# Moving input loads behind the last raw weight pieces, and two pieces into another buffer, in a fused RWKV-7 and hard-swish kernel

## The chip, the cores and the metric

The kernel runs on one core of one Trainium2 chip. The metric is the device time of one execution in microseconds (us). Three runs of the kernel before took 801.73, 801.97 and 802.9 us, so the median is 801.97 us. Separately, one execution was profiled; the views below come from that one.

A core has five engines with an instruction queue each: TensorE (PE in the views; its weight loads appear as PEld), VectorE (DVE), ScalarE (ACT), GpSimd (POOL) and SyncE (SP), which here does nothing but issue DMA transfers. Engines run their own queue in order and wait for each other by semaphores.

## The reference

The recurrence over time of four batches with eight heads of size 40, and then a feed-forward layer on its outputs:

```
for t in range(S):                                   # S = 768
    y[:, :, t] = einsum('bhd,bhde->bhe', rt, state)
    Sa = einsum('bhde,bhe->bhd', state, at)
    state = state * wt - einsum('bhd,bhe->bhde', Sa, bt) + einsum('bhd,bhe->bhde', vt, kt)
x = y.transpose(0, 2, 1, 3).reshape(B * S, H * D)    # 3072 x 320
h = x @ w_in                                         # 320 x 2048
out = (h * clip(h + 3.0, 0.0, 6.0) / 6.0) @ w_out    # 2048 x 320
```

The inputs r, k, v, w, a, b have the shape (4, 8, 768, 40), all float32. `w_in` and `w_out` come to the kernel as 8-byte numbers, seen as pairs of 32-bit words, and are turned into float32 on the chip.

## The kernel before

**Units.** Time is cut into blocks of 64 steps (BL), and two batches are worked on together (the 128 partitions are 64 steps of each). One such piece is a *unit*; there are 24, four to a group (NU = 4), so units 0 to 3 are the first group, 4 to 7 the second. For each unit, `prepare(i, F)` gives the stages that don't need the recurrent state (W, gam, A, B, F, factor, K, E, EV), and `step(i)` those that do (RT, R, VT, S, U, C, UT, rS, sn, H, y, and move, move2, which copy the output to `xt`, the operand of the feed-forward layer). A group's four units write their 32 x 32 triangular parts into one buffer `F` (tag "F", two buffers); `invert` inverts a whole group at once on VectorE, row by row, and `third_block` completes the inverse with small matmuls. These read F and write `tinv`.

**Feed-forward.** `expand` (matmuls at L1058 into PSUM, then L1073 on ACT and L1074 on DVE) and `contract` (matmuls at L1099) are a stream of small portions. `pieces(n)` takes n of them and so mixes them into PE's order.

**Weights.** `load_weights` handles 20 pieces of `w_in` and `w_out`. A raw piece is loaded by SP (L328), then ACT computes the exponent's part in three steps (L351, L353, L355), DVE the mantissa's in two (L372, L376), and DVE's L363 multiplies the two into `win`, `win2` or `wout`. ACT's result goes to one of two buffers `parts` in turn. `raw_homes` yields the place of each raw piece, and in `free` the number of the piece that has to be converted first because it had that place. The places are: a and b, the halves of a buffer with tag "F"; c, d in `wout`, e, f in `win`, g, h in `tinv`; and "x", "fb", "tt", which the inversion uses too. `limit[0]` bounds how many pieces are loaded; it becomes 20 after line 3 of the plan.

**Order.** All engines' orders are written out by hand. For the first group's steps it is the text `PLAN`: each line names stages (0sn: stage sn of unit 0), and the number behind the colon says how many conversion steps are dealt out between its matmuls and its evacuation. P and Q are the stages W and gam of units 4 and 5. From line BEGIN = 10 on, the second group's preparation (`by_twos`) runs beside it.

**Loads.** `fetch(name, i)` issues the loads of an input of unit i: two DMAs of 80 KB for w, a, b, k (L460), four of 40 KB for r, v (L457). All but the very first go through SP, whose order is the order in which the program reaches the calls. Before the change, around the end of the first group's steps, SP's order is: R of unit 3 (called in RT of unit 2), raw pieces 13 and 14, `xt` of unit 0, V of unit 5 (called in gam of unit 5), raw piece 15, R of unit 4 (called in RT of unit 3), `xt` of unit 1, raw piece 16, V of unit 4, A of unit 5, W of unit 7 (the three called after plan line 8), raw pieces 17, 18, 19, the first half of `xt` of unit 2, B and K of unit 5, and the second half of that `xt`. Then come A of unit 6, A of unit 7, W of unit 8, `xt` of unit 3, B and K of units 6 and 7, and V of units 6 and 7.

Names of the views: a wait "L924 UT" is ACT's read of the stage UT's result from PSUM; "L902 U" that of the stage U; L934 are PE's matmuls of stage rS; L476 are PE's transposes of one input of one unit.

Of the kernel before, what the change touches and what calls it, by code (L numbers as in the profile page):

```python
# [8 lines left out]
F32 = mybir.dt.float32  # L9
I32 = mybir.dt.int32  # L10
U32 = mybir.dt.uint32
# [6 lines left out]
P = 128  # L18
BL = 64
# [12 lines left out]
def kernel(  # L32
# [42 lines left out]
    nc = tc.nc  # L75
    B, H, T, D = r.shape
# [3 lines left out]
    NU = 2 * NP  # L80
    DM, DFF = moe_w_in.shape
    NJ = DFF // P
    NH = NU * H
# [8 lines left out]
    inv = ctx.enter_context(tc.tile_pool(name="inv", bufs=1))  # L92
# [48 lines left out]
    def ps_pair(*dims):  # L141
# [21 lines left out]
        out=ident[:], in_=ones, pattern=[[1, P]],  # L163
# [4 lines left out]
        out=ones[:, 0:BL], in_=ones[:, 0:BL], pattern=[[1, BL]],  # L168
# [3 lines left out]
        out=ones[BL:P, 0:BL], in_=ones[BL:P, BL:P], pattern=[[1, BL]],  # L172
# [49 lines left out]
    for i in range(3):  # L222
        t = const.tile([P, H, BL], F32, name=f"score{i}")
# [48 lines left out]
    WC = 256  # L272
# [5 lines left out]
    def raw_homes():  # L278


        raws = inv.tile([P, NH, BL], F32, name="raw", tag="F", bufs=2)
        raws = raws[:].rearrange("p h t -> p (h t)").bitcast(U32)
        places = [raws[:, n * 4 * WC:(n + 1) * 4 * WC] for n in range(2)]
        for j in (NJ // 4, 3 * NJ // 4):
            places.append(wout[:, j:j + NJ // 4, :].rearrange("p j m -> p (j m)")[:, 0:4 * WC].bitcast(U32))
        places = [x.rearrange("p (n c t) -> p n c t", n=2, t=2) for x in places]
        for c in (DFF // 4, 3 * DFF // 4):
            x = win[:, :, c:c + 2 * WC].bitcast(U32)
            places.append(x.rearrange("p n (c t) -> p n c t", t=2))
        x = tinv[:].rearrange("p h t -> p (h t)").bitcast(U32)  # L290
        for n in range(2):
            y = x[:, n * 4 * WC:(n + 1) * 4 * WC]
            places.append(y.rearrange("p (n c t) -> p n c t", n=2, t=2))
        a, b, c, d, e, f, g, h = places
        order = [g, h, a, b, c, d, e, f, a, b, c, d, "x", "fb", "tt", a, b, "fb", "tt", a]
        free = [None] * 8 + [2, 3, 4, 5, None, None, None, 8, 9, 13, 14, 15]
        left = {}
        for n, (x, before) in enumerate(zip(order, free)):
            if isinstance(x, str):
                if x not in left:  # L300
                    left[x] = inv.tile([P, L, L], F32, name=f"raw_{x}", tag=x)
                x = left[x][:].rearrange("p t s -> p (t s)").bitcast(U32)
                x = x.rearrange("p (n c t) -> p n c t", n=2, t=2)
            yield x, before
# [221 lines left out]
    def prepare(i, F):  # L526
# [25 lines left out]
        def gam_stage():  # L552

            prods, wm = o["prods"], o["wm"]
            first = start[:].rearrange("p (n i) -> p n i", i=HB + 1)[:, :, 0]
            nc.vector.reciprocal(first, prods[:].rearrange("p r m i -> p (r m) i")[:, ::-1, HB])
            back = _ap(wm[:], SCAN, [[-1, SCAN]])
            nc.vector.tensor_tensor_scan(out=back, data0=back, data1=start[:], initial=0.0,  # L558
                                         op0=ALU.mult, op1=ALU.add)
            nc.vector.memset(first, 1.0)  # L560
            gam = o["G"] = grp.tile([P, NPR, P], F32, name="gam", tag="gam", bufs=NU + 2)
            rgam = o["rg"] = placed.get(("rgam", i)) or tmp.tile([P, NPR, P], F32, name="rgam", bufs=2)
            gv = gam[:].rearrange("p r (q i) -> p (r q) i", q=2)
            rv = rgam[:].rearrange("p r (q i) -> p (r q) i", q=2)
            row = 2 * (HB + 1)

            def copy(to, x):
                if i < NU:
                    nc.scalar.activation(out=to, in_=x, func=AF.Copy)
                else:  # L570
                    nc.vector.tensor_scalar(to, x, 1.0, None, ALU.mult)

            copy(gv[:, :, 0:HB], _ap(o["wm"][:], HB + 1, [[row, NB], [-1, HB]]))
            copy(rv[:, :, HB:BL], _ap(o["wm"][:], HB + 3, [[row, NB], [1, HB]]))
            nc.gpsimd.tensor_copy(gv[:, :, HB:BL], o["prods"][:, :, 1, 0:HB])  # L575
            nc.gpsimd.tensor_copy(rv[:, :, 0:HB], o["prods"][:, :, 0, 0:HB][:, :, ::-1])
            dec = grp.tile([P, 2, 2, NPR], F32, name="dec", tag="dec", bufs=NU + 2)
            nc.gpsimd.tensor_copy(dec[:].rearrange("p m q r -> p r q m"),
                                  o["prods"][:].rearrange("p (r q) m i -> p r q m i", q=2)[:, :, :, :, HB])
            o["dec"] = dec  # L580
            if NU < i <= 2 * NU:
                fetch("V", i)
            yield from ()

# [16 lines left out]
        def f_by_32():  # L601

            f = ps_pair(NPR, BL)
            for pr in range(NPR):
                for c in range(2):
                    for q in range(2):
                        for s in range(2):
                            x = q * BL + c * L
                            y = o["bt"][half(s, D), pr, half(q)].rearrange("p (c t) -> p c t", c=2)
                            if c:  # L610
                                y = y[:, ::-1, :]
                            z = (q ^ s) * BL + c * L
                            nc.tensor.matmul(out=f[s][z:z + L, pr, :],
                                             lhsT=o["at"][half(s, D), pr, x:x + L], rhs=y,
                                             start=True, stop=True, tile_position=(s * SLOT, z))
            yield PE
            nc.scalar.activation(out=F[:, n * H:n * H + H, :].rearrange("p (s r) t -> p s r t", s=2), in_=f[2],
                                 func=AF.Copy, scale=-1.0)

        def f_by_64():  # L620

            f = ps_pair(NPR, BL)
            for pr in range(NPR):
                for q in range(2):
                    for s in range(2):
                        nc.tensor.matmul(out=f[s][half(q ^ s), pr, :],
                                         lhsT=o["at"][half(s, D), pr, half(q)],
                                         rhs=o["bt"][half(s, D), pr, half(q)],
                                         start=True, stop=True)
            yield PE  # L630
            to = F[:, n * H:n * H + H, :].rearrange("p (s r) t -> p s r t", s=2)
            for z in range(0, P, BL):
                nc.scalar.activation(out=to[z:z + L, :, :, 0:L], in_=f[2][z:z + L, :, :, 0:L],
                                     func=AF.Copy, scale=-1.0)
                for c in range(2):
                    nc.scalar.activation(out=to[z + L:z + BL, :, :, c * L:c * L + L],
                                         in_=f[2][z + L:z + BL, :, :, L - c * L:BL - c * L],
                                         func=AF.Copy, scale=-1.0)
# [185 lines left out]
    def step(i):  # L824
# [8 lines left out]
        def s_RT():  # L833
            x = turn_in(o["RN"], halves)
            yield PE
            m["RT"] = turned("RT")
            for y, z in zip(parts_of(m["RT"], halves), x):
                nc.scalar.activation(out=y, in_=z, func=AF.Copy)  # L838
            if i:
                fetch("R", i + 1)  # L840
            if fresh:
                nc.gpsimd.tensor_copy(last_dec[p][:], dec[:, 1])
                return
            scale = tmp.tile([P, 2, NPR], F32, name="scale", bufs=2)
            nc.gpsimd.tensor_tensor(out=scale[:], in0=last_dec[p][:], in1=dec[:, 0], op=ALU.mult)
            nc.gpsimd.tensor_copy(last_dec[p][:], dec[:, 1])
            nc.vector.tensor_tensor(out=st[:, :, :, 0:D], in0=st[:, :, :, 0:D],
                                    in1=_ap(scale[:], 0, [[NPR, 2], [1, NPR], [0, D]]), op=ALU.mult)
# [314 lines left out]

    third, F, group_F = [], None, []

    def prepared(i):
        nonlocal F
        if i >= NK:
            return None
        if i % NU == 0:  # L1170
            F = inv.tile([P, NH, BL], F32, name="F", tag="F", bufs=2)
            group_F.append(F)
        return prepare(i, F)

    STAGES = 9
# [108 lines left out]
    for t, line in enumerate(plan):  # L1284
# [7 lines left out]
            limit[0] = PIECES  # L1292
        if t == BEGIN - 2:
            seconds()
            fetch("V", NU)
            fetch("A", NU + 1)
            fetch("W", NU + 3)
            third.clear()
            second_group = by_twos(NU, 3, 0, 1.25)
        if t == BEGIN + 1:  # L1300

            for name in "BK":
# [162 lines left out]
```

## Time and profile before

| what | value |
|---|---|
| median of 3 runs | 801.97 us (801.73 to 802.9) |
| profiled execution | 800.6 us, span 798.6 us |
| mean granted TensorE clock of that execution | 0.957 of full speed |
| DMA rate over the span | 56 GB/s; 174215 packets, 157424 of them under 512 bytes |
| the chain that ended last | PE 72%, DVE 13%, issue 5%, DMA 4%, SP's queue 4% |

The span is the time from the first to the last instruction in the trace; what lies around it is 2.0 us. Shares of busy time are means over stages with different limits. The first 165 us are a stage of their own (preparation of the first group, its inversion, its steps and the weights' conversion); from about 175 us PE works almost without a break. In the timelines, SPq rows are DMA issues: their duration is the time that SP was taken up by issuing, not that of the transfer.

### The profile page before, as it was taken

How to read it: one execution, taken by the hardware profiler on the slowest of the kernel's cores; microseconds unless marked ns; L12 is line 12 of the kernel's file. 1: busy time of each engine (PE TensorE's matmuls, PEld its weight loads, DVE VectorE, ACT ScalarE, POOL GpSimd, SP SyncE). 2: the span in 40 equal slices, each digit the busy share in tenths (PEclk: the TensorE clock that was granted, in tenths of full speed). 3: DMA queues.
4: the chain of work that ended last, by engine and by line, in shares of the span. 5: the costliest groups of instructions: out<-in, count | busy, mean ns of one | idle time of the engine just before them, and what ended most of it. 6: DMA issues, size and time to landing. Idle time of an engine off the chain costs nothing.

```text
span 798.6 us, 35318 instructions
## 1 busy us (share of the span) xinstructions
PE 731.4 (92%) x15832; PEld 621.3 (78%) x15832; DVE 495.9 (62%) x971; ACT 320.0 (40%) x664; POOL 174.7 (22%) x318
## 2 busy tenths in 40 slices
PE   5726686999999989999999999999999999999998
PEld 4625675878778878888888888888888888888886
DVE  7897975689545699445698445898444983322210
ACT  2357864321553424452334453324444324412111
POOL 6403110320222313223124123304222202000000
PEclk9855797999999999999999999999999999999999
DMA  9683552420323321233222223213222101110000
GB/s 123 120 199 94 133 145 65 77 42 9 54 49 70 62 49 36 47 62 59 41 43 45 44 57 63 52 28 60 43 49 48 24 16 29 30 29 9 14 19 17
DMA packets 174215, 45.03 MB, mean 56 GB/s; under 512 B 157424, under 2 KB 172784, under 8 KB 174064
## 3 DMA queue, kind: packets, MB, share of 16 engines
q1 hardware_dynamic: 169760, 42.03, 27.2%
q8 instruction: 125, 2.05, 1.0%
q10 hardware_dynamic: 4304, 0.74, 0.7%
q14 instruction: 26, 0.21, 0.1%
HBM read 34.08 MB, written 3.93 MB: 48 GB/s over the span
## 4 chain that ended last, share of the span: by engine, by line
PE 72%; DVE 13%; issue 5%; DMA 4%; SPq 4%; ACT 2%; POOL 1%; DVEq 0%; ACTq 0%; POOLq 0%
PE h L1058 24%; PE o L1099 22%; PE pair L514 4%; PE pair L976 3%; DVE prod L745 3%; DVE x L751 3%; PE pair L953 2%; PE pair L486 2%; PE one L476 2%; SPq L460 2%; PE pair L898 2%; SPq L457 2%; PE pair L860 2%; PE pair L934 1%; PE pair L918 1%
## 5 line engine op out<-in xcount | busy, mean ns | idle before, releaser
L1058 PE MATMUL h<-xt,win 128*128 128x128 f32 (+1 forms) x2304 | 249.4, 282 | 3.5 <-DVE gt L1074 3.3
L1058 PEld LDWEIGHTS h<-xt,win 128*128 128x128 f32 (+1 forms) x2304 | 230.0, 191 | 20.7 <-issue 4.6
L1099 PE MATMUL o<-wout,gt 128*128 128x320 f32 x768 | 230.8, 443 | 0.0
L1099 PEld LDWEIGHTS o<-wout,gt 128*128 128x128 f32 x768 | 138.7, 190 | 50.5 <-issue 0.4
L1074 DVE SCALAR_TENSOR_TENSOR gt<-gt,h 128x512 f32<-128x512 f32 x96 | 62.0, 680 | 72.0 <-ACT gt L1073 72.0
L1073 ACT ACTIVATE gt<-h,three 128x512 f32<-128x512 f32 x96 | 62.1, 685 | 97.6 <-PE h L1058 97.2
L988 POOL TENSOR_TENSOR yg<-ys,gam 128x512 f32<-128x512 f32 x22 | 39.0, 1772 | 157.8 <-DVE ys L987 75.0
L745 DVE TENSOR_TENSOR prod<-x 128x30 f32<-128x30 f32 (+9 forms) x180 | 67.2, 373 | 8.8 <-POOL x L730 3.3
L666 POOL TENSOR_TENSOR KBt<-K,rgt 128x320 f32<-128x320 f32 x22 | 19.1, 867 | 216.7 <-ACT rgt L655 205.6
L751 DVE TENSOR_TENSOR x<-x,prod 128x30 f32<-128x30 f32 (+9 forms) x180 | 62.2, 346 | 5.5
L961 DVE TENSOR_TENSOR state<-pair,state 40x320 f32<-40x320 f32 (+1 forms) x43 | 21.0, 488 | 63.5 <-PE pair L953 37.4
L522 DVE COPY_PREDICATED score<-mask,pair 128x512 f32<-128x512 int32 x72 | 50.5, 722 | 0.9 <-PE pair L514 0.4
L987 DVE TENSOR_TENSOR ys<-pair,ys 128x512 f32<-128x512 f32 x22 | 15.2, 690 | 44.4 <-PE pair L693 22.9
L558 DVE TENSOR_TENSOR_SCAN wm<-wm,start 128x528 f32<-128x528 f32 x24 | 37.5, 1563 | 0.8
L547 DVE TENSOR_TENSOR_SCAN prods<-wm,start 128x528 f32<-128x528 f32 x24 | 30.2, 1261 | 10.3 <-ACT wm L543 10.2
L838 ACT ACTIVATE RT<-pair 128x512 f32<-128x512 f32 x22 | 13.1, 596 | 53.8 <-PE pair L486 53.8
L698 ACT ACTIVATE EV<-pair 64x320 f32<-64x320 f32 x44 | 19.0, 431 | 33.0 <-PE pair L693 22.3
L813 ACT ACTIVATE tinv<-pair 32x256 f32<-32x256 f32 x48 | 18.0, 374 | 31.1 <-PE pair L803 30.5
L1117 ACT ACTIVATE ob<-o 128x320 f32<-128x320 f32 x22 | 9.6, 434 | 49.0 <-PE o L1099 24.8
L575 POOL COPY gam<-prods 128x256 f32<-128x256 f32 x24 | 22.0, 917 | 31.4 <-DVE prods L547 30.6
L976 PE MATMUL pair<-score,KBt 64*64 64x64 f32 x1408 | 26.2, 223 | 0.2 <-issue 0.2
L864 DVE TENSOR_TENSOR RR<-pair,EV 128x320 f32<-128x320 f32 x22 | 10.7, 486 | 25.3 <-PE pair L514 25.3
(264 smaller groups left out, 1078.0 us busy)
## 6 DMA issues: line engine op xcount, KB each, us to landing
V<-in_v_dram SPq DMA_DIRECT2D x96, 40.0 KB
out_dram<-ob SPq DMA_DIRECT2D x47, 80.0 KB
R<-in_r_dram SPq DMA_DIRECT2D x92, 40.0 KB
B<-in_b_dram SPq DMA_DIRECT2D x42, 80.0 KB
K<-in_k_dram SPq DMA_DIRECT2D x42, 80.0 KB
W<-in_w_dram SPq DMA_DIRECT2D x37, 80.0 KB
A<-in_a_dram SPq DMA_DIRECT2D x37, 80.0 KB
xt<-yg SPq DMA_DIRECT2D x72, 40.0 KB
```

Source lines behind the costliest of these rows:

```text
L514: nc.tensor.matmul(out=o[i][half(q), n, :], lhsT=lhs[half(i, D), n ^ (2 * q * swap), half(q)], rhs=rhs[half(i, D), n, half(q)], start=True ...
L522: nc.vector.copy_predicated(out=x[:].rearrange("p (i h) t -> p i h t", i=2), mask=mask8, data=o[2])
L547: nc.vector.tensor_tensor_scan(out=prods[:].rearrange("p r m i -> p (r m i)"), data0=wm[:, 0:SCAN], data1=start[:], initial=0.0, op0=ALU.m ...
L558: nc.vector.tensor_tensor_scan(out=back, data0=back, data1=start[:], initial=0.0, op0=ALU.mult, op1=ALU.add)
L745: nc.vector.tensor_tensor(out=pv, in0=_ap(x[:], (i + 1) * L + i, [[L, n], [0, i]]), in1=_ap(x[:], i * L, [[0, n], [1, i]]), op=ALU.mult,)
L751: nc.vector.tensor_tensor(out=rest, in0=rest, in1=pv, op=ALU.add)
L976: nc.tensor.matmul(out=y[q][half(s), pr, :], lhsT=o[name][half(q), h * D:h * D + SLOT], rhs=m[name][half(q), 4 * rs + 2 * s + j, :], start ...
L988: nc.gpsimd.tensor_tensor(out=yg[:], in0=m["ys"][:].rearrange("p r q t -> p r (q t)"), in1=o["G"][:], op=ALU.mult)
L1058: nc.tensor.matmul(out=hp[c][:, i, :], lhsT=lhsT, rhs=rhs, start=(begun[c] == 0), stop=(begun[c] == 3 * NQ - 1))
L1073: nc.scalar.activation(out=gt[:], in_=hp[c][:], func=AF.Relu, bias=three[:], scale=1.0)
L1074: nc.vector.scalar_tensor_tensor(out=gt[:], in0=gt[:], scalar=6.0, in1=hp[c][:], op0=ALU.min, op1=ALU.mult)
L1099: nc.tensor.matmul(out=op[:], lhsT=gts[c][:, n, :], rhs=wout[:, c * HJ + r * NQ + n, :], start=((split or r == 0) and c == 0 and n == 0), ...
```

## The change

The places of pieces 15 to 19 were a, b, fb, tt, a, with the last three waiting for pieces 13, 14 and 15 to be converted. They become a, b, F0, F1, fb: the two halves of the first group's F, without a wait for another piece, and then fb, after piece 13. Four loads of inputs are taken from where they were and called after plan line 10 (A of unit 5, W of unit 7) and after plan line 12 (V of units 4 and 5, R of unit 4). So that the first group's F can still be named when the pieces are loaded, the second group's F is no longer allocated when its preparation is set up, but at its first use (`lazy_F`).

```diff
-        order = [g, h, a, b, c, d, e, f, a, b, c, d, "x", "fb", "tt", a, b, "fb", "tt", a]
-        free = [None] * 8 + [2, 3, 4, 5, None, None, None, 8, 9, 13, 14, 15]
+        order = [g, h, a, b, c, d, e, f, a, b, c, d, "x", "fb", "tt", a, b, "F0", "F1", "fb"]
+        free = [None] * 8 + [2, 3, 4, 5, None, None, None, 8, 9, None, None, 13]
...
-            if isinstance(x, str):
+            if isinstance(x, str) and x[0] == "F":
+                x = group_F[0][:].rearrange("p h t -> p (h t)").bitcast(U32)[
+                    :, int(x[1]) * 4 * WC:(int(x[1]) + 1) * 4 * WC]
+                x = x.rearrange("p (n c t) -> p n c t", n=2, t=2)
+            elif isinstance(x, str):
...
-            if NU < i <= 2 * NU:
+            if NU + 1 < i <= 2 * NU:
                 fetch("V", i)
...
-            nc.scalar.activation(out=F[:, n * H:n * H + H, :].rearrange("p (s r) t -> p s r t", s=2), in_=f[2],
+            nc.scalar.activation(out=F()[:, n * H:n * H + H, :].rearrange("p (s r) t -> p s r t", s=2), in_=f[2],
                                  func=AF.Copy, scale=-1.0)
...
-            if i:
+            if i and i != NU - 1:
                 fetch("R", i + 1)
...
+    def lazy_F():
+        made = []
+
+        def get():
+            if not made:
+                made.append(inv.tile([P, NH, BL], F32, name="F", tag="F", bufs=2))
+                group_F.append(made[0])
+            return made[0]
+        return get
+
     def prepared(i):
...
         if i % NU == 0:
-            F = inv.tile([P, NH, BL], F32, name="F", tag="F", bufs=2)
-            group_F.append(F)
+            F = lazy_F()
         return prepare(i, F)
...
         if t == BEGIN - 2:
             seconds()
-            fetch("V", NU)
+            third.clear()
+            second_group = by_twos(NU, 3, 0, 1.25)
+        if t == BEGIN:
             fetch("A", NU + 1)
             fetch("W", NU + 3)
-            third.clear()
-            second_group = by_twos(NU, 3, 0, 1.25)
+        if t == BEGIN + 2:
+            fetch("V", NU)
+            fetch("V", NU + 1)
+            fetch("R", NU)
```

SP's order after the change is: `xt` of unit 0, raw piece 15, `xt` of unit 1, raw pieces 16, 17, 18, 19, A of unit 5, W of unit 7, the first half of `xt` of unit 2, B and K of unit 5, the second half of that `xt`, V of units 4 and 5, R of unit 4, A of unit 6, and from there on as before. The orders of instructions on PE, ACT, DVE and POOL stay as they were, apart from the buffers that the conversion of pieces 17 to 19 reads.

More of the change, by code (lines that the diff above doesn't have):

```diff
@@ L630, in f_by_64 @@
             yield PE
-            to = F[:, n * H:n * H + H, :].rearrange("p (s r) t -> p s r t", s=2)
+            to = F()[:, n * H:n * H + H, :].rearrange("p (s r) t -> p s r t", s=2)
             for z in range(0, P, BL):
```

## The prediction

> **What bounds the kernel now.** I read the page first (busy shares, the 40 slices), then the timeline of each engine between 78 and 205 us, where the changed issues lie, then the stretches of 2 us with their granted clock.
>
> ```profile
> PE 731.4 (92%) x15832; PEld 621.3 (78%) x15832; DVE 495.9 (62%) x971; ACT 320.0 (40%) x664; POOL 174.7 (22%) x318
> ...
> PE   5726686999999989999999999999999999999998
> ```
>
> TensorE (PE) sets the time, and nearly all that it does not work lies in the first seven slices of 20 us. From 300 to 700 us the stretches show it busy 98.7 to 100%. So a microsecond won on PE's path before 170 us stays won, unless something else holds PE up between there and the dense part. The issues of the diff lie at 96 to 119 us. PE's timeline there (start, us, what; in brackets the idle time before it and what ended it):
>
> ```profile
> 86.90 2.41 PE L976 MATMUL lent<-score,KBt 64*64 64x64 f32 x64 [1.91 <-DVE state L961]
> ...
> 104.47 0.69 PE L934 MATMUL pair<-RT,S 40*64 40x64 f32 x32
> ...
> 112.01 1.16 PE L1058 MATMUL h<-xt,win 128*128 128x128 f32 x8 [2.68 <-DVE gt L1074]
> ...
> 116.86 4.04 PE L1058 MATMUL h<-xt,win 128*128 128x128 f32 x40
> 127.42 1.13 PE L934 MATMUL pair<-RT,S 40*64 40x64 f32 x32 [6.52 <-ACT UT L924]
> ```
>
> The longest hole is the 6.52 us up to 127.42: PE waits for ScalarE (ACT) to read UT. ACT's timeline says why that is late:
>
> ```profile
> 113.57 0.78 ACT L351 ACTIVATE parts<-raw,low 128x512 int32<-128x512 int16 x1 [1.76 <-DMA raw<-in_moe_w_out_dram]
> ...
> 115.77 0.42 ACT L902 ACTIVATE U<-pair 128x320 f32<-128x320 f32 x1
> 120.28 0.77 ACT L351 ACTIVATE parts<-raw_fb,low 128x512 int32<-128x512 int16 x1 [4.10 <-DMA raw_fb<-in_moe_w_out_dram]
> ...
> 126.79 0.58 ACT L924 ACTIVATE UT<-pair 128x512 f32<-128x512 f32 x1
> ```
>
> ACT converts the raw weight pieces 16 to 19 in program order ahead of UT, and waits 1.76 us for piece 16 and 4.10 us for piece 17. Those were issued late, since SyncE's queue (SPq) issues without a pause from 82 to 122 us:
>
> ```profile
> 96.33 2.68 SPq L457 DMA_DIRECT2D V<-in_v_dram  x4
> 99.11 0.54 SPq L328 DMA_DIRECT2D raw<-in_moe_w_out_dram  x1
> 99.76 2.61 SPq L457 DMA_DIRECT2D R<-in_r_dram  x4
> ...
> 108.65 0.53 SPq L328 DMA_DIRECT2D raw<-in_moe_w_out_dram  x1
> 109.22 3.36 SPq L457 DMA_DIRECT2D V<-in_v_dram  x4
> 112.69 1.27 SPq L460 DMA_DIRECT2D WA<-in_a_dram  x2
> ...
> 115.42 0.57 SPq L328 DMA_DIRECT2D raw_fb<-in_moe_w_out_dram  x1
> ...
> 128.65 1.72 SPq L460 DMA_DIRECT2D B<-in_b_dram  x2
> ...
> 137.86 1.34 SPq L460 DMA_DIRECT2D A<-in_a_dram  x2
> ...
> 153.33 1.57 SPq L460 DMA_DIRECT2D K<-in_k_dram  x2
> ```
>
> The reader is to see that one issue costs SP 0.6 to 0.85 us whatever it carries, so the loads of V, R, A and W stand ahead of the raw pieces by their count.
>
> **The change, part by part.** No instruction is added to or taken from PE, ACT, VectorE (DVE) or GpSimd (POOL), and their order is the same; a few carry other waits. Only SP's order and two buffers differ.
>
> *Earlier pieces.* From start to start, V of unit 5 holds SP 2.78 us (96.33 to 99.11), R of unit 4 2.66 (99.76 to 102.42), V of unit 4 3.47 (109.22 to 112.69), A of 5 and W of 7 together 2.73 (112.69 to 115.42). Piece 16 now has the first two no longer ahead: 108.65 - 5.44 = 103.21. Piece 17 has all four gone: 115.42 - 11.64 = 103.78, and piece 18 0.67 behind it. Their new home, the first group's F, is free: its last reader, the third block's matmuls (L780), ended at 76 us. In the old homes they would have waited until pieces 13 and 14 were converted, 105.65 and 108.71. Piece 19 takes the home of 13 and so issues at 105.7 to 107.8. Piece 16 landed 4.83 us after its issue (108.65 to ACT's start less the 0.09 us between), and three pieces crossed between 117 and 122.6 us, under 2 us each. So the four land by about 108, 109.5, 111 and 113 (estimate from these rows).
>
> *ACT.* L1073 ends at 111.80 and piece 16 is there: L351 starts 1.76 us earlier and its third step ends near 114.1. The next, U (L902), needs PE's L898, which ends at 114.71, so U ends at 115.13 rather than 116.19. Piece 17 starts there rather than at 120.28: 5.15 us earlier. Three pieces at the 2.17 us that they take now (120.28 to 126.79) bring UT to 121.64. DVE keeps up: piece 16's last step, held up beside POOL's L988 as now, ends near 117.2, which is when ACT wants that buffer; each later piece costs DVE 0.43 + 0.69 + 0.69 = 1.81 us, under ACT's 2.17. **PE's L934 starts at about 122.27: -5.15 us**, and PE's hole shrinks to about 1.9 us.
>
> *The clock.* The granted clock in the stretches (columns: span, PE, PEld, DVE, ACT, POOL busy with counts, clock, DMA share, GB/s):
>
> ```profile
> 86.00:88.00 2.00, 1.10 (x32) 0.95 (x32) 2.00 (x4) 1.25 (x3) 1.48 (x4) 0.65 0.37 57
> ...
> 110.00:112.00 2.00, 0.00 (x0) 0.00 (x0) 1.13 (x3) 1.81 (x4) 0.00 (x0) 1.00 0.78 242
> ...
> 126.00:128.00 2.00, 0.58 (x20) 0.58 (x24) 1.65 (x3) 1.97 (x5) 0.00 (x0) 0.50 0.00 0
> ```
>
> After the hole of 6.52 us the clock stays at 0.50 until about 134.4 us (the stretch 134 to 136 has 0.90), so L934 takes 1.13 us rather than the 0.69 of 104.47. A hole of 1.91 us (to 86.90) also halved it, until 93 us; one of 2.68 us (to 112.01) did not. So for a hole of 1.9 us both can come. Halved again, PE takes the 9.98 us from 127.42 to the transposes at 137.40 as now. At full clock, by the full-clock rows of the same work (0.51 + 0.91 + 0.67 + 1.27 + 1.0 + 2.35 = 6.7), 3.3 us more are gained: -8.4 in all. [...]
>
> *The moved loads.* V of 4 and 5 and R of 4 (12 issues) now stand behind xt of unit 2 and ahead of A of unit 6 and all that follows; A of 5 and W of 7 fall before 116 us, where SP would idle until POOL's yg, and cost nothing. The 12 cost 2.78 + 2.66 + 3.47 = 8.91 us. Now SP needs 26.25 us from B at 128.65 to the end of K of unit 7 at 154.90, of which 3.54 us (134.32 to 137.86) is waiting for PE. Without that and with the 12: 26.25 - 3.54 + 8.91 = 31.6. B, which waits for L934, starts 5.15 earlier, at 123.5; K of unit 7 is issued by 155.1, 0.2 us later than now. PE reads it at 162.20 now, at 157.05 if shifted by 5.15. So it must land in 1.95 us. The trace has no clean landing time for such a load: from below, the 1.95 us that the chain gives to an xt copy; from above 3.2 us after the end of its issue (the load of A at 2.96 us landed 3.81 after its start, with the DMA engines full). I take 2.2, nearer the low end, since the DMA share is 0.1 to 0.5 around 150 us. That is a wait of 0.25 us; the ends give 0 and 1.25. B of unit 7 is read 1.8 us earlier and issued 1.6 to 1.8 earlier, so it waits about as long. V of 4 and 5 are read at 157.04 (now), R of 4 at 199: both landed long before.
>
> *Sum:* -5.15 + 0.25 = -4.9; with the clock full the same loads stop PE, at 162.20 - (154.5 + 2.2) = -5.5. I take **-5.2 us**. The 30 us chain of DVE (168 to 199 us) and PE's own work beside it begin from this PE work and move with it. The profiled execution took 800.6 us (span 798.6 and 2.0 around it): 795.4. The three runs have the median 801.97, 1.4 above it; the forecast for the median is 801.97 - 5.2 = **796.8 us**.
>
> **Rivals.**
> - *The loads keep up and the clock stays full*: -8.4, 793.6 us. For: the hole of 2.68 us that kept the clock. Against: K of unit 7 would have to be there at 153.8. By the issue cost of the first V loads (6.00 us for 8) and the shortest A, B, K pairs (1.27), SP saves at most 2 us.
> - *SP's backlog eats more of it*: PE, stopped for K or B of unit 7, halves its clock once more and pays up to 3.3 us. -1.9, 800.1 us. For: holes near 2 us did so at 86.90. Against: these holes would be about 1 us, in dense work.
> - *The gain is hidden*: DVE's inversion chain or a later load ends at the same time as now; 802.0 us. For: that chain is on the path from 168 to 202 us. Against: it starts from L613 and F of the same PE work.
> - *Slower: the queue is late.* If the 12 moved issues are long, K of unit 7 comes later than today. It decides from a landing at 162.2, that is an issue end 4.9 us later than worked out, at 8.91 + 4.9 = 13.8 us for 12, 1.15 each. The longest V issue in the trace took 1.50: 12 x 1.50 = 18.0, 9.1 more, landing at 166.4: +4.2, 806.2 us. For: that one row, behind a raw piece. Against: the median V issue, 0.62, and the next slowest group at 0.9 each.
>
> **How the numbers follow.** Forecast 0.62 (own range 795.3 to 798.3: the landing bounds and 0.4 us of scatter), clock full with loads in time 0.10, backlog 0.16, hidden 0.07, slower 0.05. A run of this kernel tells 0.2%, 1.6 us, from no change. The first three are faster by more than that, except a part of the backlog's upper end (0.02): faster 0.86, same 0.09, slower 0.05. The range reaches to the first rival and to the backlog: 793.4 to 800.3.
>
> **What would show it.** Right: the waits of L351 for raw pieces gone, L924 near 121.6, the hole before L934 under 2.5 us, SP busy without a break from 123 to 155, PE's transposes of K and B of unit 7 near 157 with a wait under 1.5 us. Wrong: piece 17 still waited for; issues of V and R above 1 us; the gap to today closing between 150 and 205 us.

## The result and the profile after

The changed kernel takes 798.56 us in the median of 18 runs (794.62 to 802.72); the kernel before, run beside it on the same chip, 801.91 us (798.76 to 803.48). The ratio is 0.9961, 95% interval 0.9947 to 0.9975: 3.35 us faster, by the interval's ends 2.0 to 4.25. The forecast was 796.8 us, 5.2 us faster. The direction held, but about a third of the forecast gain is missing. The time lies in the stated range (793.4 to 800.3), which took in two of the rivals; it lies just outside the forecast case's own range (795.3 to 798.3).

The profiled execution took 801.08 us (span 799.0), more than 16 of the other 17 runs, so its span must not be set against the median. It was also late before the change acts: at 66 us ACT's conversion step is 0.44 us later than in the profile of before, at 88 us 0.86, at piece 14, about 107 us, 1.15. To compare traces, I therefore count from the start of ACT's first step for piece 14 (L351 before, L355 after: the change adds four lines above it, so the lines named in the prediction are 4 higher here). The busy shares and the 40 slices of the profile after:

```profile
PE 734.8 (92%) x15832; PEld 624.2 (78%) x15832; DVE 495.9 (62%) x971; ACT 320.2 (40%) x664; POOL 174.7 (22%) x318
...
PE   5726788999999989999999999999999999999998
```

The instruction counts are the same; the sixth and seventh slice (100 to 140 us) went from 6 and 9 to 8 and 9. The place where ACT waited for raw pieces, in ACT's timeline after:

```profile
114.05 0.76 ACT L355 ACTIVATE parts<-raw,low 128x512 int32<-128x512 int16 x1
...
119.19 0.44 ACT L906 ACTIVATE U<-pair 128x320 f32<-128x320 f32 x1 [2.87 <-PE pair L902]
119.52 0.77 ACT L355 ACTIVATE parts<-F,low 128x512 int32<-128x512 int16 x1
...
126.08 0.58 ACT L928 ACTIVATE UT<-pair 128x512 f32<-128x512 f32 x1
```

Both waits for pieces (1.76 and 4.10 us) are gone, and pieces 17 to 19 run without a gap. In their place ACT waits 2.87 us in U for PE's L902. PE's timeline says why that is late, and what follows; the first line is the same group of matmuls in the profile of before, the others are from after:

```profile
114.08 0.63 PE L898 MATMUL pair<-RR,tinv 64*64 64x40 f32 x32
```

```profile
108.34 1.81 PE L1062 MATMUL h<-xt,win 128*128 128x128 f32 x17
111.89 1.19 PE L1062 MATMUL h<-xt,win 64*128 64x128 f32 x7 [1.75 <-issue]
114.36 2.08 PE L1062 MATMUL h<-xt,win 128*128 128x128 f32 x8 [1.28 <-DVE gt L1078]
116.37 1.99 PE L980 MATMUL pair<-score,KBt 64*64 64x64 f32 x64
118.13 0.92 PE L902 MATMUL pair<-RR,tinv 64*64 64x40 f32 x32
...
126.71 0.69 PE L938 MATMUL pair<-RT,S 40*64 40x64 f32 x32 [2.37 <-ACT UT L928]
...
160.13 0.63 PE L480 MATMUL pair<-ident,B 128*128 128x128 f32 x4 [1.44 <-DMA B<-in_b_dram]
```

The hole of 6.52 us shrank to 2.37. But there is a new hole of 1.75 us at 110 us, put down to "issue", that is to nothing that the profile shows; the eight L1062 matmuls after it take 2.08 us (1.16 before), because the clock has halved (0.50 in the stretch from 112 to 114 us, shown further down). And PE waits 1.44 us for B of unit 7. SP's queue after:

```profile
103.24 0.53 SPq L332 DMA_DIRECT2D raw<-in_moe_w_out_dram  x1
103.81 1.05 SPq L332 DMA_DIRECT2D F<-in_moe_w_out_dram  x2
106.50 0.92 SPq L332 DMA_DIRECT2D raw_fb<-in_moe_w_out_dram  x2
107.46 1.62 SPq L464 DMA_DIRECT2D WA<-in_a_dram  x2
109.12 3.37 SPq L464 DMA_DIRECT2D WA<-in_w_dram  x2
120.89 3.10 SPq L1006 DMA_DIRECT2D xt<-yg  x4
...
134.35 5.30 SPq L461 DMA_DIRECT2D V<-in_v_dram  x8
139.69 2.59 SPq L461 DMA_DIRECT2D R<-in_r_dram  x4
...
155.89 2.12 SPq L464 DMA_DIRECT2D B<-in_b_dram  x2
158.11 1.27 SPq L464 DMA_DIRECT2D K<-in_k_dram  x2
```

Four raw pieces of 512 KB are issued within 4.2 us. Then SP idles from 112.5 to 120.9, and the 12 moved issues of V and R stand in the dense part, from 134 to 142. What the burst does to the DMA engines, from 104 to 109 us, first in the profile of before and then in that of after (the profile gives the queue q8 the kind "instruction"; each of its packets has 16 KB and took 0.88 to 1.76 us in the execution of after):

```profile
DMA packets 288, 0.17 MB, mean 35 GB/s; under 512 B 86, under 2 KB 287, under 8 KB 287
...
q8 instruction: 1, 0.02, 1.2%
```

```profile
DMA packets 1388, 1.39 MB, mean 278 GB/s; under 512 B 32, under 2 KB 1388, under 8 KB 1388
...
q1 hardware_dynamic: 1388, 1.39, 87.4%
```

In that stretch before had one packet of q8; after has none, and two in the 5 us after it. The queue brings 125 packets in the whole execution, about one for every 253 of PE's 31664 matmuls and weight loads; the next busiest engine has 971 instructions. So I took these packets for PE's code: an estimate from these counts and the name of the kind, no record says whose they are.

### The profile page after: what moved, and what is told of

It is laid out like the page before. It is cut to its first block, busy times and chain, and to the rows that moved or that the text cites. A ratio compares the mean times of both kernels' runs of the same rounds, so it can differ in the third digit from the quotient of the medians.

```text
span 799.0 us, 35314 instructions
## 1 busy us (share of the span) xinstructions
PE 734.8 (92%) x15832; PEld 624.2 (78%) x15832; DVE 495.9 (62%) x971; ACT 320.2 (40%) x664; POOL 174.7 (22%) x318
## 4 chain that ended last, share of the span: by engine, by line
PE 75%; DVE 7%; issue 6%; SPq 5%; DMA 3%; ACT 2%; POOL 1%; POOLq 0%; ACTq 0%; DVEq 0%
PE h L1062 27%; PE o L1103 23%; PE pair L518 3%; SPq L464 3%; PE pair L980 3%; PE pair L490 2%; PE one L480 2%; PE pair L957 2%; PE pair L902 2%; PE pair L864 2%; PE pair L938 1%; PE pair L922 1%; PE pair L697 1%; SPq L461 1%; DMA R<-in_r_dram 1%
## 5 line engine op out<-in xcount | busy, mean ns | idle before, releaser
L1062 PE MATMUL h<-xt,win 128*128 128x128 f32 (+1 forms) x2304 | 251.5, 283 | 4.5 <-issue 2.5
L1062 PEld LDWEIGHTS h<-xt,win 128*128 128x128 f32 (+1 forms) x2304 | 232.0, 192 | 21.6 <-issue 6.9
```

The source lines that it names most:

```text
L1062: nc.tensor.matmul(out=hp[c][:, i, :], lhsT=lhsT, rhs=rhs, start=(begun[c] == 0), stop=(begun[c] == 3 * NQ - 1))
```

## The experiments

The theory after this profile: the gain on ACT is right, and two things take some of it back. (a) The burst (four raw pieces issued almost in a row) delays a packet of q8, taken for PE's code, PE stands still and its clock halves. (b) The issues moved into the dense part make B of unit 7 late. Rivals: the hole at 110 us is chance; the two new places cause it and not the burst; what is missing was lost elsewhere.

Columns: ratio to the kernel before, run beside it on the same chip, with its 95% interval (the medians of before were 802.39 us beside e1 to e4, 802.49 beside e6, e7, e8 and after_again, 801.12 beside e9, e10 and e3_again); then from each profile the "issue" wait of PE at 110 us, start of ACT's UT from the reference point, and PE's waits for B of units 6 and 7.

| run | median us (runs) | ratio | issue wait | UT | B waits |
|---|---|---|---|---|---|
| before | 801.91 (18) | | 0 | 21.07 | 0 |
| the change | 798.56 (18) | 0.9961 (0.9947 to 0.9975) | 1.75 | 19.21 | 1.44 |
| after_again | 799.14 (12) | 0.9968 (0.9948 to 0.9988) | 2.44 | 19.57 | 0.72 |
| e1_homes_only | 799.63 (9) | 0.9965 (0.9948 to 0.9981) | 0 | 18.46 | 0 |
| e2_loads_only | 797.89 (7) | 0.9941 (0.9919 to 0.9963) | 0 | 16.03 | 0.32 |
| e3_loads_early | 797.32 (6) | 0.9938 (0.9920 to 0.9956) | 2.12 | 18.61 | 0 |
| e3_again | 796.51 (6) | 0.9947 (0.9930 to 0.9964) | 0.41 | 17.43 | 0 |
| e4_backlog_doubled | 801.96 (12) | 0.9998 (0.9981 to 1.0014) | 1.82 | 18.05 | 2.32 |
| e6_spread_and_early | 797.25 (10) | 0.9943 (0.9924 to 0.9963) | 0.39 | 16.03 | 0 |
| e7_burst_spread | 799.09 (12) | 0.9954 (0.9937 to 0.9972) | 0.60 | 17.39 | 1.57, 1.08 |
| e8_burst_dummy | 799.66 (12) | 0.9972 (0.9949 to 0.9995) | 0.44 | 16.05 | 0.40 |
| e10_dummy_doubled | 798.33 (12) | 0.9970 (0.9955 to 0.9985) | 1.79 | 19.18 | 1.62, 1.27 |
| e9_loads_between | 794.90 (6) | 0.9927 (0.9908 to 0.9945) | 0 | 16.01 | 0 |

**The change's two halves.** *e1_homes_only*: only the places F0, F1 and fb; the loads are called where they were before.

```diff
-            if NU + 1 < i <= 2 * NU:
+            if NU < i <= 2 * NU:
...
-            if i and i != NU - 1:
+            if i:
...
         if t == BEGIN - 2:
+            fetch("V", NU)
+            fetch("A", NU + 1)
+            fetch("W", NU + 3)
...
-        if t == BEGIN + 2:
-            fetch("V", NU)
-            fetch("V", NU + 1)
-            fetch("R", NU)
```

> Only the places of pieces 17 to 19 are changed; V of 4 and 5, R of 4, A of 5 and W of 7 are issued where they were before the change. My theory (the gain is that piece 17 is there sooner, whatever brings it forward): piece 17 is issued right behind 16, at about 109.2 us rather than 115.42; ACT still waits about 1.8 us for piece 16, but no longer 4.1 us for piece 17, so UT and PE's L934 come 4.1 us sooner, there is no backlog behind B of unit 5, and the time is 798 us (-4). Rival (the gain is the order of the loads; new places alone bring nothing): the wait of 4.1 us stays, 802 us.

*e2_loads_only*: the old places of the pieces, the loads moved as in the change. (They are five: A of unit 5, W of 7, V of 4, V of 5 and R of 4; the section on the change counts four.)

```diff
-        order = [g, h, a, b, c, d, e, f, a, b, c, d, "x", "fb", "tt", a, b, "F0", "F1", "fb"]
-        free = [None] * 8 + [2, 3, 4, 5, None, None, None, 8, 9, None, None, 13]
+        order = [g, h, a, b, c, d, e, f, a, b, c, d, "x", "fb", "tt", a, b, "fb", "tt", a]
+        free = [None] * 8 + [2, 3, 4, 5, None, None, None, 8, 9, 13, 14, 15]
```

> Only the five loads are moved; pieces 17 to 19 keep the old places and wait for pieces 13, 14 and 15. My theory: piece 17 is issued at 105.7, 18 at 108.7, 19 at 113.2, each lands before ACT wants it, so both waits of ACT go as with the whole change; the raw transfers come one by one and not as 2 MB at once, so PE's wait for its own instructions (1.75 us at 111.89 in the trace of the changed kernel) goes too, while the wait for B of unit 7 stays: 797.5 us, about 1 us under the changed kernel's 798.6. Rival one (the burst does nothing to PE's instructions, the wait is chance): 798.6 us. Rival two (the new places are needed, the old ones make SP wait): a wait of ACT for pieces 18 or 19 and 800 us or more.

Each half alone makes the kernel faster. e1 is 2.8 us faster, where 4 was expected: the wait for piece 17 is gone, but ACT still waits 1.41 us ahead of piece 16 (put down to DVE's L367), and V, A and W still stand ahead of piece 19, in ACT's timeline of e1:

```profile
122.65 0.75 ACT L355 ACTIVATE parts<-raw_fb,low 128x512 int32<-128x512 int16 x1 [1.81 <-DMA raw_fb<-in_moe_w_out_dram]
```

e2 is 4.5 us faster, more than the whole change in the middle of its interval, though the intervals overlap. Its raw pieces go out at 103.6, 107.3, 110.4 and 114.9 us, each when its place is free, and all are in time. So SP's order was the cause of the old waits, as the prediction has it, and the new places were not needed for the gain. PE's timeline of e2 has the forecast hole ahead of L938 and none put down to "issue" near 110 us, only the 2.68 us that before has too:

```profile
113.69 1.16 PE L1062 MATMUL h<-xt,win 128*128 128x128 f32 x8 [2.68 <-DVE gt L1078]
...
124.06 0.69 PE L938 MATMUL pair<-RT,S 40*64 40x64 f32 x32 [2.18 <-ACT UT L928]
```

**The moved loads.** *e3_loads_early*: the whole change, but V of 4 and 5 and R of 4 are called with A of 5 and W of 7 behind the raw pieces. *e4_backlog_doubled*: the whole change, and R of unit 4 loaded a second time where the moved loads stand.

```diff
             fetch("W", NU + 3)
-        if t == BEGIN + 2:
             fetch("V", NU)
```

```diff
             fetch("R", NU)
+            fetch("R", NU)
```

> The whole change, but V of 4 and 5 and R of 4 are called after plan line 10, together with A of 5 and W of 7, where SP's queue stood idle from 112.5 to 120.9 us. My theory (the 12 issues ahead of A, B and K of units 6 and 7 make PE wait for B of unit 7 and cost 1.4 to 2 us): that wait goes, V and R fill the idle time, xt of unit 2 is issued no later than 122, and the time is 797 us, 1.5 under the changed kernel. Rival (the backlog costs nothing, what is missing from the forecast is lost earlier): 798.6 us.

> The whole change, and R of unit 4 is loaded twice, so that four more issues (2.7 us of SP) stand ahead of A, B and K of units 6 and 7. My theory (backlog): PE waits 2.7 us longer for B of unit 7, 801.3 us. Rival (SP's queue has room there): 798.6 us.

e3 has no wait for B or K and is 5.1 us faster than before; e4 loses the gain, 801.96 us against 801.3 expected. The wait did not grow at B of unit 7, as expected, but stands at B of unit 6, and K of unit 7 comes 1.0 us later than before; PE's timeline of e4:

```profile
158.23 1.01 PE L480 MATMUL one<-ident,B 128*128 128x128 f32 x4 [2.32 <-DMA B<-in_b_dram]
```

The time follows the number of issues in the dense part, in both directions, as theory (b) has it; the intervals of e3 and the change overlap, those of e4 and the change don't. The same kernel as e3 once more:

> The whole change with V of 4 and 5 and R of 4 called after plan line 10, once more beside the other two: 797.3 us, ratio 0.994, no wait for B of unit 7, the issue wait of 1.5 to 2.5 us there.

It repeated the ratio (0.9947) and the absence of the B waits; but its issue wait was 0.41 us, where the first profile of the same kernel had 2.12. So that wait differs between executions of one kernel.

**The burst.** *e6_spread_and_early*: the new places, but piece 18 after 13 and 19 after 14, V of 4 and 5 called after plan line 8, A, W and R after line 10.

```diff
-        free = [None] * 8 + [2, 3, 4, 5, None, None, None, 8, 9, None, None, 13]
+        free = [None] * 8 + [2, 3, 4, 5, None, None, None, 8, 9, None, 13, 14]
...
+        if t == BEGIN - 2:
+            fetch("V", NU)
+            fetch("V", NU + 1)
...
             fetch("W", NU + 3)
-        if t == BEGIN + 2:
-            fetch("V", NU)
-            fetch("V", NU + 1)
             fetch("R", NU)
```

> The whole change with both suspected costs removed: piece 17 right behind 16, then V of 4 and 5, then piece 18 (behind the conversion of 13) and 19 (behind 14), then A of 5, W of 7, R of 4. No four raw pieces in a row, and no V or R ahead of A, B, K of units 6 and 7. My theory (the burst starves PE of instructions and costs ACT's stage U about 2 us; the backlog costs 1.4 us at B of unit 7): no PE wait put down to issue between 104 and 114 us, UT 16.0 us after ACT's first step of piece 14 (as in the loads-only kernel; before 21.1), no wait for B of unit 7, 796 us (6 under the kernel before). Rival one (the backlog alone costs): as the kernel with the loads early, 797.3. Rival two (spreading makes pieces 18 or 19 late): a wait of ACT for them and 799 or more.

797.25 us where 796 was expected, and UT at 16.03 as forecast; the issue wait fell to 0.39 but not to 0, and B is not waited for. The time is that of the first rival: no better than e3, though the burst is broken up. *e7_burst_spread* was to spread the pieces alone, and *after_again* repeats the change beside it:

```diff
-        free = [None] * 8 + [2, 3, 4, 5, None, None, None, 8, 9, None, None, 13]
+        free = [None] * 8 + [2, 3, 4, 5, None, None, None, 8, 9, None, 14, 15]
```

> The whole change, except that piece 18 waits for the conversion of 14 and piece 19 for that of 15, so the raw transfers come one by one; the moved loads stay where the change has them. My theory: no PE wait put down to issue, UT 16.0 us after ACT's first step of piece 14 rather than 19.2, the wait for B of unit 7 stays or grows: 797.5 to 798 us. Rival (the burst costs nothing, the loads-only kernel was faster by its old places): 798.6 to 799, like the changed kernel, with the issue wait.

> The whole change once more, on the same chip as the other three: 798.6 us, ratio to the kernel before 0.996; PE's wait put down to issue near 110 us and a wait of 1 to 2 us for B of unit 7 are both there again if they are not chance.

e7 missed its aim. The numbers in `free` only say where in the program the call may stand; no wait hangs on them for F0 and F1, and SP's order in its trace is that of the change, with piece 19 out at 106.2 us. It is in effect one more run of the change, and gives the like: 0.9954. *after_again* gives 0.9968 and has both waits again, 2.44 us of "issue" and 0.72 us for B.

*e8_burst_dummy* puts a burst into e2 from outside: behind piece 16 two more pieces are loaded into the first group's F, which nothing reads. *e10_dummy_doubled* loads four.

```diff
             loaded.append((out, raw))
+            if issued[0] == 17:
+                for k, (_, again) in enumerate(list(weight_pieces())[17:19]):
+                    x = group_F[0][:].rearrange("p h t -> p (h t)").bitcast(U32)[:, k * 4 * WC:(k + 1) * 4 * WC]
+                    for to, src in again(x.rearrange("p (n c t) -> p n c t", n=2, t=2)):
+                        nc.sync.dma_start(out=to, in_=src)
```

> The loads-only kernel (old places, no burst), and behind piece 16 two more transfers of 512 KB, again the data of pieces 17 and 18, into the first group's F, where nobody reads them before they are overwritten. The dependences of PE, ACT, DVE and POOL are those of the loads-only kernel; only the DMA engines have more to do between 104 and 112 us. My theory (raw bursts delay PE's instruction loads): PE waits 1.7 to 2.1 us put down to issue near 110 us, U comes about 2 us later, 799.5 to 800 us against 797.9. Rival (the place F or its semaphores made the wait): no such wait, 798 us.

> As the kernel with two dummy transfers behind piece 16, but with four (2 MB); nobody reads them. My theory (PE's instruction load stands behind the raw data on the DMA engines): the load near 107 us starts later still, PE's wait put down to issue grows from 0.44 to 2 us or more, and the time from 799.7 to 801 or more. Rival (the wait comes from the semaphores or is chance): a wait of at most 0.6 us as with two, 799.7. A caveat of both: piece 17, issued behind 2 MB, may land only by 113, still ahead of its use at 115.

The wait that e2 doesn't have appears, and grows with the bytes: 0, 0.44, 1.79 us (one profile each, and the two of e3 differ by as much; 1.7 to 2.1 us were expected of e8, 2 or more of e10). PE's timeline of e10 has the same picture as the change, although all pieces of e10 lie in the old places:

```profile
111.48 1.02 PE L1067 MATMUL h<-xt,win 64*128 64x128 f32 x7 [1.79 <-issue]
113.78 2.08 PE L1067 MATMUL h<-xt,win 128*128 128x128 f32 x8 [1.28 <-DVE gt L1083]
```

So it is the burst and not the places. In time the answer is weaker. e8's 799.66 us is the time that the theory had, but not by the theory's way: its UT came at 16.05, as in e2, so its profile has no delay there that would explain 1.8 us; and its interval touches that of e2. e10 is not slower than e8 (0.9970 and 0.9972), where over 801 us was expected. What a microsecond of this wait costs in the median is not resolved.

The records of q8 go with the burst: counted from the reference point, the packet at this place starts at 0.24 us in the profile of before (105.96 us) and at 2.58 in that of the change (109.45), 2.34 us later, and PE goes on 1.29 us after the delayed packet has ended (110.60 and 111.89). In the other runs the packets counted by stretch place it no closer: e1, e2 and e9, but e3, e4 and e10 as well, have one between 104 and 109 us (e1 issues three pieces in a row too, but only from 109.32, behind its packet). The issue wait falls into three groups: none in before, e1, e2 and e9, 0.39 to 0.60 us in e3_again, e6, e7 and e8, 1.75 to 2.44 in the change (both runs), e3, e4 and e10. In all nine profiles that have the wait it stands at the same place of PE's program, behind the 17th of the same 24 L1062 matmuls (ahead of the 1738th of all in the change). That this packet is what PE waits for is my reading of these agreements; no record names it. How busy the DMA engines are doesn't tell by itself: in e9 the data queue kept them 83.0% busy in the same 5 us (87.4% in the change), and PE had no such wait.

Holes put down to "issue" are not peculiar to the burst either. PE has two in the profile of before, of 0.25 and 1.76 us (to 34.78 and 38.03), and ahead of the burst, to 89.9 us, one of 0.70 us in after_again and one of 0.61 in e2. Near 110 us, only the nine profiles with the burst have one.

**A version with neither.** *e9_loads_between*: old places; V of 4, V of 5 and R of 4 are issued by SP right behind the pieces 16, 17 and 18, in the time in which the next piece's place isn't free yet; A of 5 and W of 7 stay behind the pieces.

```diff
             loaded.append((out, raw))
+            if 17 <= issued[0] <= 19:
+                fetch("VVR"[issued[0] - 17], (NU, NU + 1, NU)[issued[0] - 17])
...
-        if t == BEGIN + 2:
-            fetch("V", NU)
-            fetch("V", NU + 1)
-            fetch("R", NU)
```

> The old places, so that pieces 17, 18, 19 wait for 13, 14, 15, and V of 4, V of 5 and R of 4 issued in the gaps that these waits leave on SP, one behind each of pieces 16, 17 and 18. No burst and no backlog, and V and R cost SP no time that it had for anything else. My theory: no PE wait put down to issue, UT 16.0 us after ACT's first step of piece 14, no wait for B of unit 7, 796 us, the least of all. Rival (the moved V and R make pieces 18 and 19 late): ACT waits for them and the time is 798 or more.

794.90 us, 0.9927 (0.9908 to 0.9945): the best of all, 6.2 us faster than before and outside the change's interval. SP's queue in e9, where each load of V or R fills a gap between two raw pieces:

```profile
102.33 0.53 SPq L332 DMA_DIRECT2D raw<-in_moe_w_out_dram  x1
102.96 2.72 SPq L463 DMA_DIRECT2D V<-in_v_dram  x4
105.98 0.38 SPq L332 DMA_DIRECT2D raw_fb<-in_moe_w_out_dram  x1
106.40 3.59 SPq L463 DMA_DIRECT2D V<-in_v_dram  x4
110.09 0.55 SPq L332 DMA_DIRECT2D raw_tt<-in_moe_w_out_dram  x1
110.74 3.41 SPq L463 DMA_DIRECT2D R<-in_r_dram  x4
114.26 1.09 SPq L332 DMA_DIRECT2D raw<-in_moe_w_out_dram  x2
```

No issue wait near 110 us, no wait for B, UT at 16.01, and piece 17 still in time.

## Why the prediction was right in direction and too large

**What bounds the kernel, and the cause of the old hole: right.** ACT's two waits are gone, and e1 and e2, one half each, show that SP's order made them. DVE kept up, as worked out. (The issues of the raw pieces, 0.53 to 0.57 us, lie a little below the 0.6 to 0.85 us that the prediction read from its rows; no sum hangs on it.)

**The term -5.15 us was mis-sized: about -1.9 in the profile.** The step that failed is "U (L902) needs PE's L898, which ends at 114.71". That end was taken over from the trace of before as if nothing of the change touched PE there. In the changed kernel's profile the same matmuls end at 119.05, from the reference point 3.2 us later than before (12.18 and 8.99), because PE stood still for 1.75 us and then ran at half clock. Of the 3.2 us, 1.2 are there when the next eight L1062 start, since the hole ahead of them, for gt, shrank from 2.68 to 1.28 us; the other 2.0 come after it, at half clock. The windows of PE's clock after (span, PE, PEld, DVE, ACT, POOL, clock, DMA share, GB/s):

```profile
110.00:112.00 2.00, 0.25 (x5) 0.11 (x2) 1.53 (x3) 1.78 (x3) 0.00 (x0) 0.99 1.13 258
112.00:114.00 2.00, 1.08 (x7) 0.79 (x7) 0.38 (x1) 1.10 (x2) 0.00 (x0) 0.50 0.57 100
```

UT started 19.21 us behind the reference point (19.57 in the second profile), against 21.07 before and 15.92 forecast. Where the burst is missing, the forecast term is right to about 0.1 us: 16.03, 16.01 in e2 and e9. A short issue wait alone cost nothing at UT: e6 and e8, with 0.39 and 0.44 us of it, have UT at 16.03 and 16.05. In e3_again and e7, with 0.41 and 0.60 us, the clock fell to half for about 3.4 us at about 113 us as well (0.50 from 113 to 116 in e7; in e3_again by the same slower rows of PE), and UT came at 17.43 and 17.39. The prediction did work out that four pieces land by 113 us; it never asked what else the DMA engines carry meanwhile.

**The wait of 0.25 us for the moved loads was mis-sized: 1.44 and 0.72 in the two profiles, past the upper bound of 1.25 in one.** The terms on SP's side were right: from B of unit 5 to the end of K of unit 7, 31.9 us against 31.6; 8.03 us for the 12 issues against 8.91; and B of unit 7, which the prediction had waiting about as long as K, was there 2.12 us after the end of its issue, against 2.2. PE waited there first, and then no longer for K. What differs is PE's need. Before it read B of unit 7 here,

```profile
160.44 0.60 PE L476 MATMUL pair<-ident,B 128*128 128x128 f32 x4
```

33.02 us after the start of rS; in the changed kernel it would have come to it after 31.98, because the clock stayed full for part of the time. So most of the 1.44 us gives back what the clock had won (the table below has it at the same matmuls). e3 takes this wait away and is, on the mean of two runs each, 0.2% or 1.8 us ahead of the change, which the intervals don't separate; e4 adds four issues and is 2.7 us behind the mean of the change's two ratios. The prediction's rival "the backlog eats more" named this wait, with 1.9 us of gain left; the measured 3.35 lies between it and the forecast. The further halving of the clock that the rival had at this wait isn't there in the change (its clock is full from 132.4 to 173.4 us); in e4 it is.

**The clock behind the hole: neither of the two cases.** L938 ran at full clock (0.69 us), but the clock fell 2.3 us after its start and stayed at half for 3.4 us (the shares of the slices with 0.76 and 0.89):

```profile
126.00:128.00 2.00, 1.01 (x53) 0.88 (x56) 1.90 (x4) 2.00 (x5) 0.26 (x1) 1.00 0.04 8
128.00:130.00 2.00, 2.00 (x91) 1.77 (x84) 1.78 (x4) 0.30 (x1) 0.26 (x1) 0.76 0.24 41
130.00:132.00 2.00, 2.00 (x12) 0.86 (x13) 0.23 (x1) 0.00 (x0) 0.00 (x0) 0.50 0.60 100
132.00:134.00 2.00, 2.00 (x67) 1.77 (x66) 0.61 (x1) 0.00 (x0) 0.00 (x0) 0.89 0.27 56
```

From L938 to the transposes of A it took 8.72 us, where the prediction had 9.98 (half) or 6.7 (full); by the same rows before took 9.81, the prediction's 9.98 ends at a start that another view has 0.17 us later. In e3 the clock stayed full and it took 7.06. So the 3.3 us of the full-clock rival exist, but which run gets how much of them changes.

**Hidden, and slower: did not happen.** The 12 moved issues took 0.67 us each, where the last rival needed 1.15.

**"A microsecond won on PE's path before 170 us stays won, unless something else holds PE up": in the change's profiles the clock did.** PE runs the same 15832 matmuls in every kernel, so its lead over the profile of before can be read at the same matmuls, counted from the reference point (us):

| profile | start of rS | transposes of A | last transposes of K, unit 7 | end of the 48 matmuls of L1058/L1062 from 175 us |
|---|---|---|---|---|
| forecast (clock half) | 5.15 | 5.15 | 4.9 | 4.9 |
| the change | 1.86 | 2.95 | 1.42 | 0.06 |
| after_again | 1.50 | 2.31 | 1.29 | -0.08 |
| e7_burst_spread | 3.68 | 6.42 | 3.56 | 3.54 |
| e3_loads_early | 2.46 | 5.21 | 5.34 | 4.01 |
| e3_again | 3.64 | 6.38 | 6.47 | 5.11 |
| e2_loads_only | 5.04 | 5.87 | 5.21 | 3.85 |
| e9_loads_between | 5.06 | 5.91 | 6.06 | 6.07 |

The last column shows a third loss that the prediction didn't have: 1.4 us between 162 and 181 us. First the lines of before, then those of after:

```profile
172.65 0.68 PE L693 MATMUL pair<-V,score 64*64 64x40 f32 x32 [1.59 <-DVE score L522]
173.26 1.34 PE L1099 MATMUL o<-wout,gt 128*128 128x320 f32 x4
174.73 0.68 PE L693 MATMUL pair<-V,score 64*64 64x40 f32 x32
```

```profile
172.39 0.68 PE L697 MATMUL pair<-V,score 64*64 64x40 f32 x32 [1.50 <-DVE score L526]
173.00 2.14 PE L1103 MATMUL o<-wout,gt 128*128 128x320 f32 x4
175.06 1.09 PE L697 MATMUL pair<-V,score 64*64 64x40 f32 x32
```

The hole is the same, but in after the clock fell to half for 3.413 us behind it. So it did in both profiles of the change, both of e3, in e2, e6, e8 and e10 (by the last of these V matmuls, which took 1.09 us), and it did not in before, e1, e7 and e9 (0.68 us). What decides it is not shown. The prediction's own sign of being wrong, "the gap to today closing between 150 and 205 us", came true in both profiles of the change. These are single executions, the change's two slower than its median: e7, in effect the same kernel and profiled in its fastest run, kept 3.5 us. And up to 2.1 us more change hands between 181 us and the end (in e2 the lead falls to 1.71).

What is missing in the change's two profiles is, then: 3.3 and 3.7 us at rS by the burst, with the half clock behind the hole; of this the clock gives back 1.1 and 0.8 by the transposes of A, the backlog takes 1.5 and 1.0 (2.9 in e7, where more had been won), and the clock at 173 us another 1.4. In the medians the order is as the two causes have it: e3, with only the burst, has on the mean of its two runs a ratio of 0.9942, e2, with only the backlog, 0.9941, the change 0.9961 and 0.9968, and e9, with neither, 0.9927. But e6, nearly without either, has 0.9943, and of the steps only that from the change to e9 lies outside the intervals of both its runs, and that to e4 outside one. So e9 bears out that the two together cost the change what it lacks; how that divides between them is argued. A part of e9's lead may be the clock at 173 us, which its one profile shows full. Still open: what each microsecond of the issue wait costs in the median, and why one kernel's runs spread over 8 us (794.62 to 802.72 for the change), in which the differing falls of the clock may have a part.

## What to carry to other kernels

When a queue that issues loads is the cause of a wait, look for its gaps before moving loads to its end: in e9 the issues in the gaps cost nothing that its profile shows, while those in the dense part reappeared as a wait (1.44 and 0.72 us for B in the two profiles of the change). A large transfer that starts earlier need not be free even if nobody waits for the bytes (with the dummy transfers of e8 and e10 PE had waits of 0.44 and 1.79 us that e2 lacks): add up what else the DMA engines have to bring in that time, the packets of the instruction queue included. A duration taken from the old trace holds in the new one only if the engine isn't disturbed by what the change starts earlier (here 8.99 us became 12.18). And where two kernels run the same instructions in the same order, the lead at the same instruction, place by place, shows where a gain is won and where it is lost again.

## What the runs showed of the hardware

- With some 2 MB issued within about 4 us (q1 at 87.4% of all DMA engines' time from 104 to 109 us in the change), a packet of the queue of kind "instruction" started 2.34 us later than in the profile of before, and TensorE stood still for 1.75 us, 2.44 in the second profile, put down to "issue". That TensorE waited for this packet is my reading; no record names it.
- Two issues of 80 KB behind the burst took 3.37 us, at 109 us in the change (3.15 in after_again), where the shortest pairs of the same execution took 1.27. The pair ahead of them, at 107.46 us, took 1.62, so what makes an issue longer was not shown.
- The granted clock's recorded stretches at full and at half speed last whole multiples of 3.413 us in the profiles of before and of the change (3.413, 6.827, 10.240, 13.653 and longer ones); only the last is cut short, by the end of the trace. A hole's length alone doesn't tell whether the clock falls: in the change it fell 0.07 us after the end of a hole of 1.75 us (to 111.89), in e2 it stayed at 1.00 for the next 10 us behind one of 2.68 us (to 113.69), and after the holes of 2.16 to 2.38 us ahead of rS it fell about 2 us later in both profiles of the change (2.3 us in the first), in e2, e6, e8 and e9, but not in the two of e3, in e7 and e10 (PE's matmuls of RT and UT behind the hole take 0.67 us there, 0.82 to 1.13 in the others).
